# Four one-bank PSUM tiles in place of two two-bank tiles for the products of a kernel's second network, with a new instruction order

## The chip, the cores and the metric

The kernel runs on one core of a Trainium2 chip. The metric is the device time in microseconds (us) of one execution, and the time of a kernel is the median over its runs. The engines are TensorE (PE: matmuls; PEld is its weight load), VectorE (DVE), ScalarE (ACT), GpSimd (POOL) and SyncE (SP, which issues every DMA here). Matmuls write PSUM, a memory of eight banks; one bank holds 128 x 512 fp32. DVE and ACT read PSUM; POOL works on SBUF only.

## What is computed

Windowed attention feeds a first gated network, and that a second one; only the second is changed.

```python
# x: 1536 tokens x 512, from the first network
h = x @ w_in                       # 512 -> 2048
relu6 = np.clip(h + 3.0, 0.0, 6.0)
g = h * relu6 / 6.0
return (g @ w_out).astype(np.float32)   # 2048 -> 512
```

## The kernel before

Every matmul is done in two-part fp32: an operand is split into a high part and a remainder (`split`, lines 286 to 325: ACT or DVE copies the high part, POOL or DVE subtracts), and three matmuls of 128 x 512 give one product. The tokens are three chunks of 512. The second network goes in four rounds of four f-tiles (128 of the 2048 hidden columns each). In a round, chunks 0 and 1 go two f-tiles at a time through a fast scheme with seven products in place of eight (`strassen`): a product is six matmuls into one PSUM bank (`product`, line 806), and DVE at once adds the bank to a sum in SBUF (`plus`, line 889; the first is a copy, lines 894 and 895). Chunk 2 goes plainly (`single2`, line 937): two products of twelve matmuls into the two halves of one tile. So there are 56 products of six and 16 of twelve, 72 in all, and four banks for them. `act2` is the gate: ACT `Relu` into `t` (line 818), DVE `min` and multiply (819), ACT copy to the high part of `g` (821), POOL or DVE the remainder (825). For chunk 2 it takes both halves, 128 x 1024, in one instruction each. `second2` (line 848) multiplies `g` by the output weights into the banks `y0` to `y3`, three matmuls a time, and DVE adds those to `part` (863). `convert` and `weights2` (lines 305 to 313, 790) turn float64 weights, loaded by DMA, into fp32 and form differences of them.

In the first network `first_product` (line 637) and `second_product` (654) do the same jobs, with another gate (lines 701 to 745); `evac` (672) and 679 pass its result on. Attention is in lines 349 to 603.

The four product banks are two tiles, `hb0` and `hb1`, each of two banks (`pair_of`). The framework that places semaphores knows tiles: an instruction that writes or reads a tile is kept in order with the accesses to it that were recorded ahead of it. The planner inside the kernel (`Plan`) keeps its books by single banks, `("h", 0)` to `("h", 3)`; it decides nothing about semaphores.

The order is a table: `ORDER` lists all operations in the order in which they are given out, each engine runs its own in that order, and `PICK` says for an operation that can run on several engines which one does it.

Of the kernel before, what the change touches and what calls it, by code (L numbers as in the profile page):

```python
# [22 lines left out]
P = 128  # L23
# [6 lines left out]
N = 512  # L30
# [33 lines left out]
    "#P%-'##M$$$X#Q$#%.&3%3&1&W%5&,#R#Y#S%4#L%0%/%6%8&*%1'K%X'I%7%;%9%R&V&+%<%:%Y&2%=&'&-&>#.'J&4&.*X'L&5"
    "&/&?'M#T$%&@&D'D'N'$&A&(&I(,&X'%&E';+.&F#/&G&B)8&H*Y':+$&J&K#U*Z')&L&C&M&N+%+2&6&P&O&Q'*+/+#&R'<+&'."
    "+3+<+0&Z&S'++1'/+4+'&T+((-',+5'&+)'0+=(/(.'1+*'2+J)#+6''+@'-'((H++'5+A+>'3+7'6+?+,'=+B(M+8+-,$+C'V(N"
    "(%+K'>'A'O+D+9(O'B+N(I+E(J+L,#+F'4+M+O+Z+:'?'7+G,(+;+Q'@+Y(P+P'8+X+H'9'W+R,2(&+I(',5'C+S'X'E(Y(Q'Y(K"
    "'Z(L,4):'G,%)9,D(#,&'F,3),+T(T(R($)',F)-+U).(:,G(Z,',6(((U'P,+)(()))(S'R(0'Q+V'S(V(1+W,7(2)/,),E(W,:"
    ",W(X(;1L(*,V,*)0(<)$)*,;)+(='T,H(>'U,,)%(?)&)>(@(3,<)1,8)3)2,Y)4)C,X,-)5,.,I(+,L,Z)?)D,9)E(A)6,/(4)7"
    ",J)@,M,=,K);,N-#,>(6)A-4,0)Q,?)O-&,1)=(5)<,O)B)F-'-1-51M,@-3)G-0,A,P)H-(-$-8-2(7,B)J(D-F)I,C)Z,Q-%(8"  # L70
    ',R-)-9-E(9)U)K-D*#,S*$-B-:(B)L-*(C-+-X,T*.-,1Z-G*%)P-6,U1S---J(E)M-T-H-Y-C1O(F-I*/-K-U1N)N.$-W(G-L-.'
    ")R-7-M-/2).%.6-;*0)T-N*&-<)V)S*9)W)X2%)Y-V.&*)-=.0**-O.:*'-P./*(2,.1.7->*4*+1T-Q..*:*,*5-?.H-R1P-Z-@"
    ".;.2*-.#.3-A.4*1.I*6*;.5.8.<.L.E*<-S*2.'.G.9.(.F*=.M.=.W*7.)2#.Z.>*3*G*8.N.?.*.X/&.@.D/#.A*@*L.Y.+.V"
# [125 lines left out]
def tile_kernel(ctx, tc, qT, kT, kw, vw, vt, w1, w2, av, bv, masks, ident, blk, out):  # L199
# [22 lines left out]
    sp = [ExitStack() for _ in range(2)]  # L222
# [536 lines left out]
    def bank_at(n):  # L759
        return pair_of(n // 2)[:, n % 2, :]  # L760
# [50 lines left out]
    def act2(src, reads, in_psum, two, g, gk):  # L811

        n = t_used[0] % 4
        t_used[0] += 1 + two
        a, v = n // 2, (slice(0, 2) if two else n % 2)
        t = t2[a][:, v]
        tk = [("t", a, w) for w in ((0, 1) if two else (n % 2,))]
# [3 lines left out]
        add(ACT, 0.96 if two else 0.53, lambda: nc.scalar.activation(g[:, 0], t, AF.Copy), tk, gk)  # L821
        for w in range(1 + two):
            def rest(eng, w=w):
                ts, gs = (t[:, w], g[:, :, w]) if two else (t, g)
                eng.tensor_tensor(out=gs[:, 1], in0=ts, in1=gs[:, 0], op=ALU.subtract)  # L825

            add(POOL, 1.26, lambda f=rest: f(nc.gpsimd), tk[w:w + 1], gk[w:w + 1], port=True,
                more=[(DVE, 0.61, lambda f=rest: f(nc.vector), True)])
# [40 lines left out]
    def strassen(r, m):  # L869
# [241 lines left out]
```

## Time and profile before

| | us |
|---|---|
| median of 3 runs (lowest, highest) | 600.57 (599.98, 600.9) |
| the profiled execution: its own time | 601.33 |
| its span, first to last instruction | 599.5 |
| PE busy in the span | 584.6 (98%) |
| DVE busy | 496.5 (83%) |
| ACT busy, POOL busy | 352.2, 288.5 |

Busy time of PE is that of matmuls, which overlap, so what counts is the pace from one start to the next. The profiled execution took 0.76 us more than the median.

### The profile page before, as it was taken

The page shows a single profiled execution, that of the slowest core. Times are in us where ns is not written, and L with a number is a line of the kernel's source. Part 1 is how long each engine was busy: PE and PEld are TensorE (multiplying, and loading weights), DVE is VectorE, ACT ScalarE, POOL GpSimd, SP SyncE. Part 2 cuts the span into 40 slices and gives each one's busy share as a digit, 9 for nine tenths or more (in the row PEclk, how much of TensorE's full clock was granted, in tenths as well). Part 3 has the DMA queues.
Part 4 walks back from the last instruction along what each step waited for, and adds up shares of the span by engine and source line. Part 5 has one row for each costly group of instructions (what it writes and reads, how often), then busy time and mean ns, then how long its engine had stood idle before and what let it go on. Part 6 is the DMA issues. An engine that isn't in the chain of part 4 may idle for free.

```text
span 599.5 us, 9595 instructions
## 1 busy us (share of the span) xinstructions
PE 584.6 (98%) x3613; PEld 466.1 (78%) x3613; DVE 496.5 (83%) x874; ACT 352.2 (59%) x637; POOL 288.5 (48%) x269
## 2 busy tenths in 40 slices
PE   8999999999999999999999999999899999999997
PEld 4477888888888888888888778787678888778886
DVE  5999999989999999978999889747797868568653
ACT  3999989999677777846665454324640433233410
POOL 2688655462554535465666645242523066254400
PEclk9999999999999999999999999999899999999999
DMA  8967631501331313100001300320412024002005
GB/s 314 361 238 240 229 113 68 172 1 34 107 105 36 106 36 134 43 2 0 35 1 37 112 29 28 112 71 1 140 35 106 1 72 140 1 1 71 0 2 210
DMA packets 17982, 53.10 MB, mean 89 GB/s; under 512 B 2272, under 2 KB 2784, under 8 KB 17936
## 3 DMA queue, kind: packets, MB, share of 16 engines
q1 hardware_dynamic: 17936, 52.49, 25.3%
q8 instruction: 28, 0.46, 0.3%
q14 instruction: 18, 0.15, 0.1%
HBM read 48.55 MB, written 3.15 MB: 86 GB/s over the span
## 4 chain that ended last, share of the span: by engine, by line
PE 82%; DVE 8%; POOL 4%; issue 2%; ACT 2%; DMA 1%; SPq 0%; DVEq 0%; POOLq 0%; ACTq 0%
PE y L654 22%; PE y L848 15%; PE hb L637 15%; PE hb L806 11%; PE hs L637 8%; PE hb L937 6%; PE hs L574 2%; PE hs L507 2%; PE hs L591 2%; DVE q L889 1%; DMA mask_sb<-in_masks 1%; POOL g L825 1%; DVE raw L313 1%; POOL wt L325 1%; DVE t L819 1%
## 5 line engine op out<-in xcount | busy, mean ns | idle before, releaser
L654 PE MATMUL y<-g,wt 128*128 128x512 f32 x576 | 138.9, 392 | 0.0
L654 PEld LDWEIGHTS y<-g,wt 128*128 128x128 f32 x576 | 107.0, 188 | 22.2 <-POOL g L745 0.3
L848 PE MATMUL y<-wt,g 128*128 128x512 f32 x480 | 118.0, 391 | 0.3 <-DVE wt L325 0.2
L848 PEld LDWEIGHTS y<-wt,g 128*128 128x128 f32 x480 | 90.4, 189 | 20.0 <-DVE wt L325 0.5
L637 PE MATMUL hb<-xx,wt 128*128 128x512 f32 x384 | 89.6, 389 | 0.0
L325 POOL TENSOR_TENSOR wt<-raw,wt 128x512 fp32r<-128x512 f32 x38 | 53.3, 1407 | 63.9 <-ACT wt L286 47.2
L637 PEld LDWEIGHTS hb<-xx,wt 128*128 128x128 f32 x384 | 72.0, 188 | 15.3 <-DVE t L737 0.3
L286 ACT ACTIVATE wt<-raw 128x512 fp32r<-128x512 f32 x55 | 36.4, 670 | 40.9 <-DVE raw L313 16.0
L305 POOL TENSOR_SCALAR raw<-raw 128x512 f32<-128x512 f32 x50 | 38.2, 774 | 44.6 <-DMA raw<-in_w 44.3
L309 ACT ACTIVATE raw<-raw 128x512 f32<-128x512 f32 x62 | 40.3, 668 | 30.4 <-POOL raw L305 29.7
L825 POOL TENSOR_TENSOR g<-t,g 128x512 fp32r<-128x512 f32 x21 | 29.5, 1411 | 53.3 <-ACT g L821 50.8
L821 ACT ACTIVATE g<-t 128x512 fp32r<-128x512 f32 (+1 forms) x32 | 23.2, 735 | 47.3 <-PE y L848 33.8
L313 DVE SCALAR_TENSOR_TENSOR raw<-raw 128x512 int32<-128x512 int32 x62 | 47.2, 765 | 3.2 <-ACT raw L309 2.7
L717 POOL TENSOR_TENSOR q<-q,u 128x512 f32<-128x512 f32 x28 | 38.6, 1392 | 23.2 <-ACT u L707 12.6
L806 PE MATMUL hb<-wt,wt 128*128 128x512 f32 x192 | 48.6, 393 | 0.9 <-DVE q L889 0.8
L637 PE MATMUL hs<-xx,wt 128*128 128x512 f32 x192 | 48.0, 398 | 0.0
L937 PE MATMUL hb<-xx,wt 128*128 128x512 f32 x192 | 46.5, 394 | 0.7 <-DVE q L889 0.5
L745 POOL TENSOR_TENSOR g<-t,g 128x512 fp32r<-128x512 f32 x22 | 31.7, 1445 | 26.5 <-ACT g L739 22.5
L937 PEld LDWEIGHTS hb<-xx,wt 128*128 128x128 f32 x192 | 36.4, 191 | 9.3 <-DVE q L889 1.2
L806 PEld LDWEIGHTS hb<-wt,wt 128*128 128x128 f32 x192 | 35.6, 188 | 10.2 <-issue 0.9
L806 PE MATMUL hb<-xx,wt 128*128 128x512 f32 x144 | 37.7, 398 | 5.2 <-DVE q L889 3.1
L863 DVE SCALAR_TENSOR_TENSOR part<-y,part 128x512 f32<-128x512 f32 x36 | 24.2, 685 | 22.4 <-PE y L848 22.4
(174 smaller groups left out, 1100.2 us busy)
## 6 DMA issues: line engine op xcount, KB each, us to landing
raw<-in_w SPq DMA_DIRECT2D x62, 512.0 KB, 4.3
vv<-in_vw SPq DMA_DIRECT2D x6, 512.0 KB, 7.3
out<-part SPq DMA_DIRECT2D x12, 256.0 KB, 2.9
k<-in_kT SPq DMA_DIRECT2D x4, 384.0 KB, 4.3
q<-in_qT SPq DMA_DIRECT2D x6, 256.0 KB, 7.8
e<-in_kT SPq DMA_DIRECT2D x4, 384.0 KB, 6.6
raw<-in_vt SPq DMA_DIRECT2D x3, 512.0 KB, 6.8
e<-in_vw SPq DMA_DIRECT2D x3, 512.0 KB
```

The costliest lines, as they stand in the source:

```text
L286: nc.scalar.activation(out_, in_, AF.Copy)
L305: eng.tensor_scalar(out=hif, in0=hif, scalar1=CAP, scalar2=-CAP, op0=ALU.min, op1=ALU.max)
L309: add(ACT, 0.58, lambda: nc.scalar.activation(hif, hif, AF.Prelu, scale=REBIAS, alpha=2.0 ** 32), [kr], [(kr, 1)])
L313: add(DVE, 0.61, lambda: nc.vector.scalar_tensor_tensor(out=lo, in0=hi, scalar=3, in1=lo, op0=ALU.logical_shift_left, op1=ALU.bitwise_or), ...
L325: eng.tensor_tensor(out=to()[:, 1], in0=src, in1=to()[:, 0], op=ALU.subtract)
L637: mm(ps, lt, rt, start=(k == 0), stop=(k == 11))
L654: mm(y, lt, rt, start=(i == 0 and j == 0), stop=(i == HALF - 1 and j == 2))
L717: eng.tensor_tensor(out=q2[a][:, w], in0=q2[a][:, w], in1=u2[:, w], op=ALU.mult)
L806: mm(bank_at(bank_), left(lp, kk), right(rp, kk), start=(j == 0), stop=(j == 5))
L825: eng.tensor_tensor(out=gs[:, 1], in0=ts, in1=gs[:, 0], op=ALU.subtract)
L848: mm(yb[d], lt, rt, start=(j == 0 and e == 0), stop=(j == QUART - 1 and e == 2))
L937: mm(pair_of(a)[:, u, :], w_at(n)[:, lp, kk * P:(kk + 1) * P], x_of(2)[:, rp, kk, :], start=(j == 0), stop=(j == 11))
```

## The change

The banks become four tiles `hc0` to `hc3` of one bank each, made where the second network first touches a pair, after the pair tile is closed. Chunk 2's gate is done for each f-tile by itself. `PICK` and `ORDER` are replaced whole; a line of each stands for them.

```diff
 PICK = (
-    '0001230000110000000010000000000011111011001100000100010011000000000000000001001000101001100000000000'
+    '0000230000000000001100111010000000011100001100000000000001000000110000000101110000001010000000000010'
...
 ORDER = (
-    "###)#4#(#;#$#6#2#0#8#%%>#9%Z#5#&#:#7%E#'#3#<#1#?#V$&%?#W#@$(%@$'$.&#%A#*$7%B$)$/&%$0%F$9#=%L%G$H$*$1"
+    "###(#4#)#;#$#2#6#0#8#%%>#9#:#5#&%E#3#<#'#7#W#1%Z#V$&%?#?#B$(%@$7$'$.%A%F$8#=$)#@$9#A%L%H$Y%G$*$/%B$0"
...
@@ pair_of
-            hq = ctx.enter_context(tc.tile_pool(name=f"hq{a}", bufs=1, space=PSUM, reuse_waits="tile", side=SIDES[a]))
+            hq = hs2[a].enter_context(tc.tile_pool(name=f"hq{a}", bufs=1, space=PSUM, reuse_waits="tile", side=SIDES[a]))
...
     def bank_at(n):
-        return pair_of(n // 2)[:, n % 2, :]
+
+        def make():
+            hs2[n // 2].close()
+            hr = ctx.enter_context(tc.tile_pool(name=f"hr{n // 2}", bufs=1, space=PSUM, reuse_waits="tile", side=SIDES[n // 2]))
+            return [hr.tile([P, N], F32, name=f"hc{2 * (n // 2) + u}") for u in range(2)]
+
+        return keep(("hc", n // 2), make)[n % 2]
...
-    def act2(src, reads, in_psum, two, g, gk):
+    def act2(src, reads, in_psum, g, gk):
...
-        add(ACT, 1.02 if two else 0.55, lambda: nc.scalar.activation(t, src(), AF.Relu, bias=lnb[:, 2:3]), [*reads, "lnb"], tk)
-        add(DVE, 1.14 if two else 0.61, lambda: nc.vector.scalar_tensor_tensor(
+        add(ACT, 0.5 if in_psum else 0.62, lambda: nc.scalar.activation(t, src(), AF.Relu, bias=lnb[:, 2:3]), [*reads, "lnb"], tk)
+        add(DVE, 0.61, lambda: nc.vector.scalar_tensor_tensor(
...
-                        mm(pair_of(a)[:, u, :], w_at(n)[:, lp, kk * P:(kk + 1) * P], x_of(2)[:, rp, kk, :],
+                        mm(bank_at(2 * a + u), w_at(n)[:, lp, kk * P:(kk + 1) * P], x_of(2)[:, rp, kk, :],
...
-        act2(lambda: pair_of(a), [("h", 2 * a), ("h", 2 * a + 1)], True, 1, g2[b], [("g", b, u) for u in range(2)])
         for u in range(2):
-            second2(r, 2, 2 * m + u, (g2[b][:, :, u, :], [("g", b, u)]))
+            place_ = g_place()
+            act2(lambda u=u: bank_at(2 * a + u), [("h", 2 * a + u)], True, *place_)
+            second2(r, 2, 2 * m + u, place_)
```

In the changed kernel lines 806, 848, 889 and 937 are 812, 850, 891 and 939; lines 818, 819, 821 and 825 are 822, 823, 825 and 828; 790 is 796.

**First place, PE in the first round of the second network.** `wt1`, `wt2`, `wt6` and `wt7` hold sums of activations, `wt0` and `wt5` differences of weights, `xx0` to `xx2` the three chunks. Before, from the product with `wt1`:

```order
L806 MATMUL hb0_2020<-wt1_471,wt0_360 128x512 x6
L806 MATMUL hb0_2020<-xx1_117,wt0_360 128x512 x6
L806 MATMUL hb0_2020<-xx0_115,wt3_463 128x512 x6
L806 MATMUL hb1_1964<-wt2_600,wt9_2000 128x512 x6
L806 MATMUL hb1_1964<-wt7_1238,wt5_1075 128x512 x6
L806 MATMUL hb0_2020<-wt1_471,wt5_1075 128x512 x6
L848 MATMUL y0_81<-wt8_1958,g1_80 128x512 x3
L806 MATMUL hb1_1964<-xx0_115,wt3_463 128x512 x6
```

The first three go to halves 1, 0 and 1 of `hb0`. Now, at the same products:

```order
L812 MATMUL hc0_3208<-xx1_117,wt0_361 128x512 x6
L654 MATMUL y2_83<-g0_79,wt5_1061 128x512 x3
L654 MATMUL y3_84<-g0_79,wt5_1061 128x512 x3
L654 MATMUL y0_81<-g0_79,wt5_1061 128x512 x3
L654 MATMUL y1_82<-g0_79,wt5_1061 128x512 x3
L812 MATMUL hc3_3160<-wt2_411,wt9_1990 128x512 x6
L812 MATMUL hc1_3209<-xx0_115,wt3_463 128x512 x6
```

Each bank has a name of its own, and twelve matmuls of the first network have moved in between.

**The same place on DVE.** Before, the additions that read those products:

```order
L325 TENSOR_TENSOR wt5_1075<-raw1_71,wt5_1075 128x512
L889 TENSOR_TENSOR q1_77<-hb0_2020,q0_76 128x512
L889 TENSOR_TENSOR q1_77<-hb1_1964,q1_77 128x512
L672 SCALAR_TENSOR_TENSOR part12_118<-y1_82,part12_118 128x512
L889 TENSOR_TENSOR q0_76<-hb1_1964,q0_76 128x512
L889 TENSOR_TENSOR q1_77<-hb0_2020,q1_77 128x512
```

The second row reads the product with `wt1` (half 1 of `hb0`), the last the product with `xx1` (half 0). Now:

```order
L891 TENSOR_TENSOR q0_76<-hc3_3160,q0_76 128x512
L891 TENSOR_TENSOR q1_77<-hc1_3209,q0_76 128x512
L891 TENSOR_TENSOR q0_76<-hc0_3208,q0_76 128x512
L325 TENSOR_TENSOR wt2_411<-part0_116,wt2_411 128x512
```

The additions stand together, and none shares a tile with a later product.

**Second place, PE and DVE where chunk 2 has its first turn.** PE before, from the last products of the Strassen pair:

```order
L806 MATMUL hb1_1964<-xx1_117,wt5_1075 128x512 x6
L848 MATMUL y1_82<-wt9_2000,g1_80 128x512 x3
L937 MATMUL hb0_2020<-xx2_119,wt8_1958 128x512 x12
L937 MATMUL hb0_2020<-xx2_119,wt9_2000 128x512 x12
L937 MATMUL hb1_1964<-xx2_119,wt4_663 128x512 x12
```

PE now:

```order
L939 MATMUL hc0_3208<-xx2_119,wt8_1956 128x512 x12
L939 MATMUL hc1_3209<-xx2_119,wt9_1990 128x512 x12
L812 MATMUL hc2_3159<-wt2_411,wt4_667 128x512 x6
L850 MATMUL y3_84<-wt9_1990,g1_80 128x512 x3
L812 MATMUL hc3_3160<-xx1_117,wt5_1061 128x512 x6
L939 MATMUL hc2_3159<-xx2_119,wt3_463 128x512 x12
```

Two Strassen products now stand between those of chunk 2, and `hc2` is written again nine matmuls after its last product. DVE now, from the read that frees `hc1` to the one that frees `hc2`:

```order
L891 TENSOR_TENSOR q0_76<-hc1_3209,q0_76 128x512
L828 TENSOR_TENSOR xx1_117<-t0_74,xx1_117 128x512
L311 TENSOR_SCALAR raw3_73<-raw3_73 128x512
L823 SCALAR_TENSOR_TENSOR t0_74<-t0_74,q0_76 128x512
L313 SCALAR_TENSOR_TENSOR raw2_72<-raw2_72 128x512
L325 TENSOR_TENSOR wt8_1956<-raw1_71,wt8_1956 128x512
L796 TENSOR_TENSOR raw1_71<-raw2_72,raw1_71 128x256
L325 TENSOR_TENSOR wt9_1990<-raw2_72,wt9_1990 128x512
L891 TENSOR_TENSOR u_78<-hc2_3159,u_78 128x512
```

Seven instructions of other jobs stand between the two reads.

## Rows read from the trace of the kernel before

**Rows 1.** Page, part 1: busy us (share of the span) x instructions.
```profile
PE 584.6 (98%) x3613; PEld 466.1 (78%) x3613; DVE 496.5 (83%) x874; ACT 352.2 (59%) x637; POOL 288.5 (48%) x269
```

**Rows 2.** Busy time by stretch: first network, its end, second network.
```profile
core 0: us, PE busy (x) PEld busy (x) DVE busy (x) ACT busy (x) POOL busy (x), PEclk, DMA share, GB/s
60.00:310.00 250.00, 250.00 (x1598) 205.15 (x1597) 234.29 (x388) 192.97 (x332) 134.71 (x118) 1.00 0.22 73
310.00:340.00 30.00, 30.00 (x134) 24.86 (x133) 26.89 (x35) 18.18 (x25) 18.98 (x15) 1.00 0.07 20
340.00:582.00 242.00, 234.98 (x1012) 189.42 (x1011) 177.47 (x256) 92.38 (x140) 95.82 (x85) 0.99 0.17 57
```

**Rows 3.** Timeline of PE: start us, us, matmuls; in brackets idle before, releaser.
```profile
309.30 12.40 PE L654 MATMUL y<-g,wt 128*128 128x512 f32 x54
321.54 1.52 PE L806 MATMUL hb<-xx,wt 128*128 128x512 f32 x6
...
339.22 1.52 PE L806 MATMUL hb<-xx,wt 128*128 128x512 f32 x6
341.53 1.67 PE L806 MATMUL hb<-xx,wt 128*128 128x512 f32 x6 [0.78 <-DVE q L889]
343.54 4.50 PE L806 MATMUL hb<-wt,wt 128*128 128x512 f32 x18 [0.34 <-DVE q L889]
...
349.76 1.65 PE L806 MATMUL hb<-xx,wt 128*128 128x512 f32 x6 [1.04 <-DVE u L889]
```

**Rows 4.** Timeline of DVE, the same place.
```profile
340.78 1.42 DVE L889 TENSOR_TENSOR q<-hb,q 128x512 f32<-128x512 f32 x2 [2.21 <-PE hb L806]
```

**Rows 5.** Waits of PE from 300 us on: us in total, times, longest us.
```profile
PE hb L806 <- DVE q L889: 3.9, 5, 2.1
PE hb L806 <- DVE u L889: 2.0, 2, 1.0
...
PE y L848 <- DVE wt L325: 0.2, 1, 0.2
```

**Rows 6.** Busy time by stretch, columns as in rows 2.
```profile
426.00:429.00 3.00, 3.00 (x10) 2.33 (x9) 1.90 (x4) 1.53 (x3) 1.15 (x2) 0.61 0.44 157
429.00:432.00 3.00, 3.00 (x12) 2.38 (x12) 3.00 (x6) 2.96 (x5) 1.18 (x1) 0.82 0.12 44
```

**Rows 7.** Groups by form: count | busy us, mean ns of one | idle before, its releasers.
```profile
L313 DVE SCALAR_TENSOR_TENSOR raw<-raw 128x512 int32<-128x512 int32 x62 | 47.2, 765 | 3.2 <-ACT raw L309 2.7
L311 DVE TENSOR_SCALAR raw<-raw 128x512 int32<-128x512 int32 x62 | 36.9, 604 | 1.8 <-DMA raw<-in_w 1.7
L325 DVE TENSOR_TENSOR wt<-raw,wt 128x512 fp32r<-128x512 f32 x40 | 33.0, 827 | 5.1 <-ACT wt L286 4.6
L889 DVE TENSOR_TENSOR q<-hb,q 128x512 f32<-128x512 f32 x35 | 23.8, 684 | 19.3 <-PE hb L806 13.9 <-PE hb L937 3.5 <-ACT u L894 1.8
L819 DVE SCALAR_TENSOR_TENSOR t<-t,q 128x512 f32<-128x512 f32 x22 | 19.8, 905 | 0.5 <-ACT t L818 0.4
L825 DVE TENSOR_TENSOR g<-t,g 128x512 fp32r<-128x512 f32 x19 | 14.9, 792 | 0.5 <-ACT g L821 0.4
L790 DVE TENSOR_TENSOR raw<-raw,raw 128x256 f32<-128x256 f32 x10 | 5.8, 581 | 6.5 <-POOL raw L790 4.2 <-POOL wt L325 2.3
L819 DVE SCALAR_TENSOR_TENSOR t<-t,hb 128x1024 f32<-128x1024 f32 x8 | 9.7, 1216 | 4.9 <-ACT t L818 4.9
L818 ACT ACTIVATE t<-hb,lnb 128x1024 f32<-128x1024 f32 x8 | 9.0, 1119 | 9.2 <-DVE g L825 6.3 <-PE hb L937 2.0 <-POOL g L825 0.9
L821 ACT ACTIVATE g<-t 128x1024 fp32r<-128x1024 f32 x8 | 8.5, 1059 | 27.5 <-PE y L848 27.5
L821 ACT ACTIVATE g<-t 128x512 fp32r<-128x512 f32 x24 | 14.8, 627 | 19.8 <-DVE t L819 13.5 <-PE y L848 6.3
```

**Rows 8.** Waits of PE over the whole span, columns as in rows 5.
```profile
PE y L507 <- DVE stat L552: 1.8, 1, 1.8
PE hs L349 <- DVE z L347: 1.2, 1, 1.2
```

More of the change, by code (lines that the diff above doesn't have):

```diff
@@ L64 @@
[L64 to L73, printed above, removed]
@@ new lines @@
+    "+<&S+3(-+''/(/+1(.&T#U+('B+4'&'++=+)'0+5',+*'-+J+@'1''+6'2'((H++'5+A+>'3+7'6+?+,'=+B(M(I+-,$+C'V'>+8"
+    "'D+K(%+D+9'O'4+E+L'7+F+N+M(N+:+X+O'8(O,#+G(J+Q+;+Y'W,%'A+R+Z(P'Y,&'?'X,4'@'9'C+H(&,5(Z'Z,('P)#,2+I('"
+    ")8'E(#(K+P(L(Q,3'G($'Q,E'F),(T(:,G(():(0(R(U+S,D(S'R,F)'+T(V'S+U(1,6()+V)()-,'(*).+W))(W'T(;)*)/,),X"
+    "(2,:(X,Y(<(=)0)$,+,*)+(>'U,H)%,,)&,7(+(3)>,;,-,8(A)1)3(?,V)2)4(@,L,W,<)C)5)?,.,/,Z,9)6,I)@)D(6)E,0)7"
+    ",J,=,M,K)A,>);,N)F,?,1,O-4)<)Q-#)O-&,@1Z)B)G)9)=(B-',P-1,A(C-2-(-5-$)J-8)P(D-3(4-%1L-0(5,Q)H,B-F-9)I"
@@ new lines @@
+    ',C)K-:-),R)Z(E(7-B-*,S)L-J-+-E,T*#-,-G-C,U)M(8-X-K)U-6)N--*$*%-7-D(9-Y)R.$)V-L)W1S-H-..%1M-;-U)X1O-I'
+    "(F)S-W-<-T2%1N(G)T.6-M*&)Y2)-=*.-N*0-/*9-V->-O*'.1-?*(*).7-P...:-Q.0***:.&*/*;*4./-Z1P*+.8.;-R.H.#*<"
+    ".<-@*,-A.'*-*5.22*1V*1.31T.(.4*6.L.Z*=*21U*3*G-S.).I*@*7.F/#.**8.5.X.+/&.E.9*L/'.D.M*>.J.W2#.=.V.K.>"
+    '*H*M.N.G.,*?*A.Y*I.?2$/4*N.O.@.-.P.A*O.Q*B/5.R/$.S/3*E.B/%/(*F/1*C*J2&/8/2/6.T/F/9*K*P*D.C/)2,/*/7*S'
+    "/0/+*T.U2+*Q/C1W*R/G/E/,/;*U/-/J/H/D/</I*V/W1Q*W/V1X/:1R/B/./K/X/M/=2I2'///N2-/>2./Y/L/O/?/P/@/U0&/Q"
@@ new lines @@
+    "0#2(0*052L2W0'/R0+0(0,/S0%060)2J/A0-2/0./T2X3&2K0/0$1Y0G0900080C2P/Z2Y010D0:070H020F0=0<0I0E0;030>0?"
+    "2Z0J0R3)2M0K3#2N0L0@0S2O3$040A3'0M3%0U1$0N0T3X1(1%0X3J0Y0O1)1&143(1*3Y2Q0Q1'132R0B1+0P4#0V1,3*0Z1=1-"
+    "0W1A1#1>1.153K181?161/1<1:1B10193Z1@11203L1C121D3M2S171E4$222T211F2U4%3+1G3,1H1;2:4&4'263N2>3-2V4U1I"
+    '3O1J1K2;2?3.3P2=2<4G2@253Q3;293?4X3/3<232A3>3@242B273A4V323=302C284H3B332D31374(4I342E4W353C4Y364J4.'
+    '2F4K3D382G4L393E4M4)414/3F2H:<4*3G3R4+3S3T5+4Z4,484-5#3H5$4<:R42493I5,3U3:4:4=3V4;4>43553W465945564N'
@@ new lines @@
+    "5.4?5:40584@475;5/5%504A5754534B:=5<445&4O5-4C5=514Q524D:U5>5D4F5?:S4E:T5@5E4P5'5A4R:?5B5(6%5N5R5O4S"
+    "5S6&:>4T5P5C:C5T5H:@6?5I5)5L5Q5*6;5G5U6@5F6<:Y5J5V:V5M6=5W5K6*6>6A6'6.:Z:D6B6)5X6(6C6,5Y;#6-6+655Z6J"
+    '6D6#686$6/6E606K616F627+6T6G6U6H7,6I696V6X6W6Y6O75;$6M:F79766Z6Q6L787:7#7.72777;7$6S707%7<6N6R637&7='
+    "6P747'667-:E647(716:7D7)7>7*7?7E:A7@:B:G8%:J:H7N:I7O7R:K8&:L;%:M7S7Q7T7/8767737P:N7I7A:O7F7U;(7G7C7B"
+    "7K7V7J887H8;7W7M8:7L8<8(898=8)8,;)7X8>8'8*7Y8?8-8+;+7Z818G8/828$8@838A8F8#8B:$:*9'8P:+:0:,8T8Q8U9(;*"
@@ L105 @@
+    "E=E(GYELF=EMG=EGF?E<F8EFE,G;G>FUE6G<E7GEEOF9GVGFF:E>G?GIH%FXEHE?EIF@GCG@EQGDGXH#ESFAGNH$EPFYG'H'I,FZ"
+    'G#GZGGH,H-EUH(G$H&G%H*GJETGKGPGHH.GLGTH/ENGOG(I-G*G)H)G&H0H+G+H4H?G,H8GSI.H9I>H5ERH1H2GMH3GQG-H>GRHB'
+    'H:H=H6H;HHI6HCH<H7H@HNHDHRI/I?I7HJHLIHHOIIHAHSHFI8HPI@I9I0HWIAI1HMHVI#HZHQI(HUHYHTI&HXI*IBI3ICI$IJI;'
+    "IKI%I4I+HII2HKI5I)HGI<I'HEI:IEI=IFINIMITIDIRIUILISIGIPIOIQIVIW"
 )
@@ L221, in tile_kernel @@
     yb = [pp.tile([P, N], F32, name=f"y{i}") for i in range(4)]
-    sp = [ExitStack() for _ in range(2)]
+    sp, hs2 = [[ExitStack() for _ in range(2)] for _ in range(2)]
     hp = [sp[i].enter_context(tc.tile_pool(name=f"hp{i}", bufs=1, space=PSUM, side=SIDES[i])) for i in range(2)]
@@ L809, in product, with rest @@
         add(PE, 1.362, go, reads, [("h", bank_)], fresh=(("h", bank_),))
-    def act2(src, reads, in_psum, two, g, gk):
+    def act2(src, reads, in_psum, g, gk):
         n = t_used[0] % 4
[L814 to L817, printed above, removed]
-        add(ACT, 1.02 if two else 0.55, lambda: nc.scalar.activation(t, src(), AF.Relu, bias=lnb[:, 2:3]), [*reads, "lnb"], tk)
-        add(DVE, 1.14 if two else 0.61, lambda: nc.vector.scalar_tensor_tensor(
-            out=t, in0=t, scalar=6.0, in1=src(), op0=ALU.min, op1=ALU.mult), reads, tk, port=not in_psum)
[L821 to L828, printed above, removed]
+        t_used[0] += 1
+        t, tk = t2[n // 2][:, n % 2], [("t", n // 2, n % 2)]
+        add(ACT, 0.5 if in_psum else 0.62, lambda: nc.scalar.activation(t, src(), AF.Relu, bias=lnb[:, 2:3]), [*reads, "lnb"], tk)
+        add(DVE, 0.61, lambda: nc.vector.scalar_tensor_tensor(
+            out=t, in0=t, scalar=6.0, in1=src(), op0=ALU.min, op1=ALU.mult), reads, tk, port=not in_psum)
+        add(ACT, 0.53, lambda: nc.scalar.activation(g[:, 0], t, AF.Copy), tk, gk)
+        def rest(eng):
+            eng.tensor_tensor(out=g[:, 1], in0=t, in1=g[:, 0], op=ALU.subtract)
+        add(POOL, 1.26, lambda: rest(nc.gpsimd), tk, gk, port=True, more=[(DVE, 0.61, lambda: rest(nc.vector), True)])
     def temp_place():
@@ L909, in strassen @@
         first = [g_place() for _ in range(2)]
-        act2(lambda: c11, k11, False, 0, *first[0])
-        act2(lambda: c12, k12, False, 0, *first[1])
+        act2(lambda: c11, k11, False, *first[0])
+        act2(lambda: c12, k12, False, *first[1])
         if m == 0:
@@ L914, in strassen @@
             for e in range(2):
-                act2((lambda: c21, lambda: c22)[e], (k21, k22)[e], False, 0, *second[e])
+                act2((lambda: c21, lambda: c22)[e], (k21, k22)[e], False, *second[e])
             for e in range(2):
@@ L920, in strassen @@
             for e in range(2):
-                act2((lambda: c21, lambda: c22)[e], (k21, k22)[e], False, 0, *second[e])
+                act2((lambda: c21, lambda: c22)[e], (k21, k22)[e], False, *second[e])
             for e in range(2):
@@ L1027, in tile_kernel, with bank_now @@
     second_network()
+    def bank_now(kind, n):
+        if kind == "y":
+            return yb[n]
+        return bank_at(n) if ("hc", n // 2) in made else pair_of(n // 2)[:, n % 2, :] if ("hb", n // 2) in made else hs[n]
     with tc.manual_schedule():
@@ L1038, in tile_kernel @@
                 for _ in range(times):
-                    mm(yb[n] if kind == "y" else bank_at(n) if ("hb", n // 2) in made else hs[n], z[:, :P], z, start=True, stop=True)
+                    mm(bank_now(kind, n), z[:, :P], z, start=True, stop=True)
             plan.ops[i][2]()
```

66 lines of the change are left out of this document (25 added, 41 removed).

## The prediction

> **What bounds the kernel now.** The page's first part says that PE is busy 98% of the span, the next engine, DVE, 83% [rows 1]. Such a busy share hides drawn-out matmuls, so I read pace instead. On the timeline of PE, 54 matmuls take from 309.30 to 321.54 us, 12.24 us or 0.2267 us each [rows 3]; that is the pace at which PE runs when nothing holds it. Then the stretches: from 60 to 310 us PE has no idle time at all, and from 310 to 340 none either [rows 2]. In the second network, 340 to 582 us, 1012 matmuls took 242.0 us; at pace they need 1012 x 0.2267 = 229.4 us [rows 2, 3]. So **12.6 us are lost there**, more than the 7.0 us by which PE's busy time falls short of the stretch.
>
> The waits of PE say on what: 3.9 and 2.0 us in seven waits of a product (L806) for a DVE addition (L889), and 0.2 us for a weight [rows 5]. They understate the loss. The block at 339.22 has six matmuls and should hand over at 340.58; the next starts at 341.53, which is 0.95 us late, with 0.78 named. That one needs 1.36 us and has 2.01 until the next, 0.65 late with 0.34 named [rows 3]. And after the longest wait, 2.1 us, the granted clock was 0.61 and 0.82, so part of those 6 us ran at the lower of the two levels, 1.2 GHz; 22 matmuls took 6.0 us instead of 5.0, another 1.0 us [rows 6].
>
> Why is the addition late? Take the first wait, with the order of before at the first place. The product with `wt1` goes to one half of `hb0` and ends when the block with `xx1` begins, at 339.22. DVE then stands idle, 2.21 us in all, and starts the addition that reads it only at 340.78, which is when the matmuls with `xx1`, into the *other* half, have ended (339.22 + 1.52 = 340.74) [rows 3, 4]. PE's next product starts when this addition is over. So both sides wait for the neighbour's bank: the tile has two banks and one history. The group of additions has the same reading in sum: 19.3 us of DVE idle time ahead of them, 13.9 and 3.5 of it put down to products [rows 7]; much of this is plain waiting for work, so it prices nothing. Read from the built program, 21 of the 72 products wait for a read of the other half of their tile, and 20 reads wait for a later product into the other half. In the changed one none does.
>
> **The change part by part.**
>
> *Four tiles.* This takes away the wait for the neighbour. At most it returns 12.6 us. What stays is a bank's own handover: DVE reads it in 0.684 us [rows 7], with 0.04 us to start (340.74 to 340.78 above), so some 0.8 us or 3.5 matmuls when DVE is free at once. Counted in the new order, no bank that an addition has to free is written again sooner than 6 matmuls (1.36 us) after its last product, and 5 of those 60 rewrites come within 12 (2.7 us); before, 4 did. PE is safe there if DVE is on time, and DVE runs in order. The second place is such a case. From the end of the read that frees `hc1` DVE has L828, L311, L823, L313, L325, L796, L325 and the addition to do: 0.79 + 0.60 + 0.91 + 0.77 + 0.83 + 0.58 + 0.83 + 0.68 = 5.99 us at the means of the same operations [rows 7]. PE, from its start on `hc1` to its next product into `hc2`, has 12 + 6 + 3 + 6 = 27 matmuls, 6.12 us. The two meet within 0.13 us, so one instruction that is late by half its length makes PE wait. I let each of the five tight rewrites cost one foreign instruction's lateness of 0.55 us (an estimate: the lightest two in that list are 0.58 and 0.60), 2.7 us in all. From below the bound is nothing; from above it is the whole 12.6 us, 0.175 us on each of 72 products.
>
> *Chunk 2's gate by single f-tiles.* Eight pairs of instructions become sixteen on each engine. DVE: 16 x 0.684 (the nearest read of one bank) less 9.7 is +1.2 us. ACT's copy: 16 x 0.627 less 8.5 is +1.5 us. ACT's `Relu` on one bank has no row; it lies between half the wide one, 0.56, and the wide one, 1.12 us, and the copy's narrow form costs 0.59 of its wide one, so I take 0.66 us, +1.6 us (bounds 0 and +8.9) [rows 7]. The cover is slack: ACT works 92.4 of 242.0 us here and DVE 177.5 [rows 2]; in a stretch of 232 us they would be at 41% and 77%. Charged: nothing; if DVE had no slack, 1.2 us. In return the first half's gate can begin after its own product, 12 matmuls or 2.7 us earlier, and frees its bank by itself.
>
> *Order and picks.* PE has the same matmuls in both programs, product by product, and as many that only fill (25). By count DVE gives six of the multiplications of line 717 to POOL in the first network and takes seven clamps of line 305 from it; PE had no idle time there, so nothing is to be won. In the attention part the planner issues scores and loads in another sequence. PE's waits there are 1.8 and 1.2 us [rows 8]: the first could go or double, the second waits for the first memset and stays. I take 0, bounds -1.8 and +1.8. The end has the same shape: one output bank after another, an addition, a store.
>
> **Sum.** 12.6 - 2.7 = 9.9 us less: 601.33 - 9.9 = 591.4 us for an execution like the profiled one, which stood 0.76 us above the median of the runs shown. So 590.7 us.
>
> **The rivals.**
>
> *A, the handover is late more often.* The additions wait on ACT and POOL as well as on PE, and without the forced pauses DVE has less time to catch up. For it: the spare 0.13 us above, and DVE at 90% just ahead, 26.9 of 30 us [rows 2]. Against it: over 242 us DVE has a quarter free. If half the loss stays, 6.3 us, the time is 601.33 - 6.3 - 0.76 = 594.3; the case reaches from 593.5 to 599.4.
>
> *B, nothing changes.* The products took turns on four banks before as well, and if DVE's own lateness were the cause, tiles would not matter: 600.6 us. The Trainium skill (Perfetto Trace Analysis, section "Matmuls") says that independent groups should rotate through different PSUM banks so that the evacuation of one overlaps the next group's matmuls; by that rule alone this kernel was already right. The trace disagrees: DVE was idle, not late, ahead of the addition at 340.78 [rows 4].
>
> *C, slower.* Place: the first network, where DVE works 234.3 of 250 us, 94% [rows 2]. The new table arranges its gates anew; if they come late, PE, which lost nothing there, loses. It decides from 9.9 us on, 0.2 us on each of the 48 f-tile steps. If DVE came to idle as much again as its 15.7 us, all on PE's path, the time would be 590.7 + 15.7 = 606.4 us. For it only the small reserve; against it, that DVE's load there gets lighter on balance of the counts above.
>
> *D, more than forecast.* No rewrite late and 1.8 us won at the start: 601.33 - 12.6 - 1.8 - 0.76 = 586.2; the case is everything below 588.
>
> **How the numbers follow.** Forecast (588 to 593.5) 0.62, A 0.20, D 0.07, B 0.04, C 0.07. From 587 to 597 lie the forecast's own range, some 0.14 of A and 0.04 of D, together 0.8; the range takes in the bound of no late rewrite (588.0) and of half the loss with 1.8 us lost at the start (596.1). A measurement of this kernel can tell about 0.2%, 1.2 us, from no change: faster 0.62 + 0.20 + 0.07 = 0.89, same 0.04, slower 0.07.
>
> **What would show it.** Right: in the second network about 2.7 us above 0.2267 us a matmul; no long wait of a product on an addition, and DVE starting an addition when its own product ends; no dip of the granted clock there; ACT's narrow `Relu` near 0.66 us and neither ACT nor DVE nearer to full; the first network still without idle time on PE. Wrong: products still waiting, now with DVE busy ahead of the addition (A); the same waits with DVE idle (B); PE idle between 60 and 310 us (C).

## The result and the profile after

The changed kernel takes 589.87 us (median of 4 runs, 588.89 to 591.61) beside 600.28 us for the kernel before (4 runs, 599.48 to 600.9) on the same chip: a ratio of 0.983, 95% interval 0.9802 to 0.9859. The profiled execution took 589.21 us, with a span of 587.4 us; before it was 601.33 and 599.5.

The page's first part after the change, which answers to [rows 1]:

```profile
PE 578.6 (98%) x3608; PEld 466.6 (79%) x3613; DVE 494.4 (84%) x887; ACT 348.5 (59%) x648; POOL 294.7 (50%) x272
```

PE's share is 98% both times, so it tells nothing of the gain. The stretches do; columns as in [rows 2], the last one cut where the program now ends:

```profile
60.00:310.00 250.00, 249.91 (x1605) 204.83 (x1595) 231.63 (x375) 190.81 (x331) 154.46 (x133) 1.00 0.22 73
310.00:340.00 30.00, 30.00 (x134) 24.70 (x133) 29.59 (x40) 16.22 (x22) 17.97 (x16) 1.00 0.08 24
340.00:572.00 232.00, 232.00 (x1025) 192.12 (x1024) 176.29 (x282) 93.34 (x156) 82.53 (x70) 1.00 0.17 59
```

In the second network PE has no idle time and the clock is at its full level: 1025 matmuls in 232.0 us, which is the pace (1025 x 0.2267 = 232.4). The first network is as tight as before. Of the waits of PE over the whole span only some at the start are left, the two largest of them here. None is on a product bank; before there were eight, the seven of [rows 5] and one of a product of chunk 2 (L937, 0.5 us):

```profile
PE hs L1045 <- issue: 1.4, 4, 0.9
PE hs L349 <- DVE z L347: 1.2, 1, 1.2
```

PE's timeline, with the first product, the second place and the last output block (the brackets that [rows 3] had are gone):

```profile
322.46 1.55 PE L812 MATMUL hc<-xx,wt 128*128 128x512 f32 x6
...
353.13 5.60 PE L939 MATMUL hc<-xx,wt 128*128 128x512 f32 x24
358.57 1.52 PE L812 MATMUL hc<-wt,wt 128*128 128x512 f32 x6
359.93 0.84 PE L850 MATMUL y<-wt,g 128*128 128x512 f32 x3
360.61 1.52 PE L812 MATMUL hc<-xx,wt 128*128 128x512 f32 x6
361.97 2.88 PE L939 MATMUL hc<-xx,wt 128*128 128x512 f32 x12
...
570.05 13.76 PE L850 MATMUL y<-wt,g 128*128 128x512 f32 x60
```

Two rows of this view give a measure that is the same for every kernel below: the time from the first product of the second network to the start of the last output block. Here it is 570.05 - 322.46 = 247.59 us. Between them lie 1092 matmuls in the new order (1089 in the old, whose last block has 63); at 0.22667 us each [rows 3] they need 247.52 us, so 0.1 us is lost. Before, from 321.54 [rows 3] to 581.47 us, it was 259.93, of which 13.1 lost. That is 13.0 us won; the first product begins 0.92 us later; 12.1 us is the difference of the spans.

The groups by form that answer to [rows 7]:

```profile
L891 DVE TENSOR_TENSOR q<-hc,q 128x512 f32<-128x512 f32 x35 | 23.5, 683 | 7.9 <-PE hc L812 7.6
L823 DVE SCALAR_TENSOR_TENSOR t<-t,hc 128x512 f32<-128x512 f32 x16 | 10.7, 681 | 4.7 <-ACT t L822 4.7
L822 ACT ACTIVATE t<-hc,lnb 128x512 f32<-128x512 f32 x16 | 10.7, 678 | 9.2 <-PE hc L939 5.8 <-DVE g L828 1.9 <-POOL g L828 1.4
L825 ACT ACTIVATE g<-t 128x512 fp32r<-128x512 f32 x40 | 25.0, 628 | 49.4 <-PE y L850 43.4 <-DVE t L823 3.1 <-DVE u L891 2.9
```

The additions of this form take what they took, but DVE's idle time ahead of them is 7.9 us instead of 19.3, and none of it is for a product of chunk 2 any more. The narrow `Relu` takes 0.678 us.

### The profile page after: what moved, and what is told of

The parts are those of the page before. It is cut to its first block, busy times and chain, and to the rows that moved or that the text cites. A ratio compares the mean times of both kernels' runs of the same rounds, so it can differ in the third digit from the quotient of the medians.

```text
span 587.4 us, 9645 instructions
## 1 busy us (share of the span) xinstructions
PE 578.6 (98%) x3608; PEld 466.6 (79%) x3613; DVE 494.4 (84%) x887; ACT 348.5 (59%) x648; POOL 294.7 (50%) x272
## 4 chain that ended last, share of the span: by engine, by line
PE 94%; DMA 2%; DVE 1%; SPq 1%; issue 1%; POOL 0%; ACT 0%; DVEq 0%
PE y L654 23%; PE y L850 22%; PE hb L637 15%; PE hc L812 13%; PE hs L637 8%; PE hc L939 7%; PE hs L591 2%; PE hs L507 2%; PE hs L574 1%; DMA mask_sb<-in_masks 1%; DMA k<-in_blk 1%; SPq L280 1%; DVE s L520 0%; POOL s L549 0%; PE hs L434 0%
## 5 line engine op out<-in xcount | busy, mean ns | idle before, releaser
L637 PE MATMUL hb<-xx,wt 128*128 128x512 f32 x384 | 89.5, 389 | 0.0
L325 POOL TENSOR_TENSOR wt<-raw,wt 128x512 fp32r<-128x512 f32 x44 | 62.4, 1425 | 51.0 <-DVE wt L322 30.4
L637 PEld LDWEIGHTS hb<-xx,wt 128*128 128x128 f32 x384 | 72.1, 188 | 15.0
L717 POOL TENSOR_TENSOR q<-q,u 128x512 f32<-128x512 f32 x34 | 46.2, 1368 | 23.8 <-ACT u L707 14.4
L825 ACT ACTIVATE g<-t 128x512 fp32r<-128x512 f32 x40 | 25.0, 628 | 49.4 <-PE y L850 43.4
L812 PE MATMUL hc<-wt,wt 128*128 128x512 f32 x192 | 47.4, 389 | 0.0
L939 PE MATMUL hc<-xx,wt 128*128 128x512 f32 x192 | 45.6, 389 | 0.0
L939 PEld LDWEIGHTS hc<-xx,wt 128*128 128x128 f32 x192 | 36.0, 188 | 7.5
L812 PEld LDWEIGHTS hc<-wt,wt 128*128 128x128 f32 x192 | 36.0, 188 | 7.5
L637 PEld LDWEIGHTS hs<-xx,wt 128*128 128x128 f32 x192 | 35.1, 188 | 7.7 <-issue 0.2
```

What stands on the lines that cost most here:

```text
L325: eng.tensor_tensor(out=to()[:, 1], in0=src, in1=to()[:, 0], op=ALU.subtract)
L637: mm(ps, lt, rt, start=(k == 0), stop=(k == 11))
L717: eng.tensor_tensor(out=q2[a][:, w], in0=q2[a][:, w], in1=u2[:, w], op=ALU.mult)
L812: mm(bank_at(bank_), left(lp, kk), right(rp, kk), start=(j == 0), stop=(j == 5))
L939: mm(bank_at(2 * a + u), w_at(n)[:, lp, kk * P:(kk + 1) * P], x_of(2)[:, rp, kk, :], start=(j == 0), stop=(j == 11))
```

## The experiments

**Theory 1**: two banks in one tile are kept in order with each other, and this is the loss. **Theory 2**: the new order and picks make the gain, and the tiles alone do nothing. **Theory 3** (rival A): the handover of a bank is late anyway, so little is to be had. Each run stands beside the kernel before on its own chip.

### Tiles and order, crossed

`e1_pair_new_order` keeps the new order, the new picks and the split gate, but the four banks are halves of two tiles again:

```diff
...
 def bank_at(n):
-    def make():
-        ...
-    return keep(("hc", n // 2), make)[n % 2]
+    return pair_of(n // 2)[:, n % 2, :]
```

> The changed kernel with one thing undone: the four product banks are halves of two tiles again; the new order, the new picks and the gate by single f-tiles stay. If the shared tile is the cause, the loss comes back, 12 us or so, since the new order was laid out for separate banks too: 598 to 605 us, with products waiting for DVE additions, DVE idle ahead of them, and some 10 us or more lost in the second network. If the new order and picks are the cause, it stays at about 590 us. If the single gate is, the same.

`e2_four_old_order` has the four tiles and the split gate, with the table of before; the two halves of each gate stand one behind the other where the wide one stood:

```diff
 PICK = (
-    '0000230000000000001100111010000000011100001100000000000001000000110000000101110000001010000000000010'
+    '0001230000110000000010000000000011111011001100000100010011000000000000000001001000101001100000000000'
...
```

> The old order and the old picks with the four tiles; each wide operation of the gate stands as its two halves, one behind the other, in the old place. If the shared tile is the cause, most of the loss is gone here as well: 588 to 593 us, and PE keeps its pace in the second network. If the new order is the cause, about 600 us. The start is the old one, so PE's first large matmul begins at about 39.6 us.

`e3_pair_old_order` has both edits, so that of the change only the split gate is left.

> The old order, the old picks and the two shared tiles, with the gate by single f-tiles alone. If the shared tile is the cause: about as before, 598 to 603 us, since the narrow gate's extra 1 to 3 us on DVE and ACT are covered and its halves still share a tile. If the narrow gate itself gives the gain, 590 to 595 us.

The stretch is that from the first product to the last output block, read from PE's timeline; lost is what it has above its matmuls at pace.

| kernel | tiles | order | stretch, us | lost, us | median, us | ratio to before |
|---|---|---|---|---|---|---|
| before | two | old | 259.93 | 13.1 | | |
| e3 | two | old | 260.38 | 13.5 | 601.04 | 0.9992 (0.9981 to 1.0003) |
| e1 | two | new | 260.05 | 12.5 | 602.65 | 1.0022 (1.0006 to 1.0038) |
| e2 | four | old | 247.70 | 0.9 | 590.54 | 0.9814 (0.9795 to 0.9834) |
| changed | four | new | 247.59 | 0.1 | 589.87 | 0.983 (0.9802 to 0.9859) |

With the same tiles, the order changes the stretch by 0.5 us at most; from two tiles to four, 12 to 13 us go in either order. Theory 2 falls: the new order on shared tiles is 0.2% slower than the kernel before, the old order on four tiles has the whole gain. In e1 the waits of PE from 300 us on are as follows (L933 is `single2`, L885 the additions, L890 and L891 the copy that a sum begins with, on ACT and on DVE, L817 the gate's `min` and multiply):

```profile
PE hb L933 <- DVE q L885: 2.5, 3, 1.4
PE hb L806 <- DVE t L817: 2.0, 2, 1.6
PE hb L806 <- DVE q L885: 1.0, 2, 0.5
PE hb L806 <- ACT q L890: 0.8, 1, 0.8
PE hb L806 <- DVE u L891: 0.6, 1, 0.6
```

These are nine waits with 6.9 us named, at other places than in [rows 5], for 12.5 us lost. The other side of it is the waits of DVE from 320 to 590 us:

```profile
DVE q L885 <- PE hb L806: 9.8, 8, 3.0
...
DVE q L885 <- PE hb L933: 5.1, 2, 3.8
```

DVE waits 14.9 us for products, and PE waits for DVE's reads: that both wait for each other is what one history for two banks does. DVE's idle time by itself shows nothing. In the changed kernel the first of these rows is 8.1 us and in e2 it is 12.5, and in neither is a wait of PE for an addition named from 300 us on; the row of e2:

```profile
DVE q L891 <- PE hc L812: 12.5, 8, 5.4
```

### One pair shared, one apart

`e4_one_pair` shares a tile between banks 2 and 3 only:

```diff
...
 def bank_at(n):
+    if n // 2 == 1:
+        return pair_of(1)[:, n % 2, :]
...
```

> The changed kernel with banks 2 and 3 as halves of one tile and banks 0 and 1 separate. If the loss belongs to the shared tile, a part near half of what the two pairs cost: 593 to 599 us, and every long wait of a product is on the tile that is shared. If what counts is something else that the shared tiles bring about, such as a load on DVE, the waits fall on the separate banks as well.

It took 597.77 us, a ratio of 0.9937 (0.9922 to 0.9952). The stretch is 254.94 us (323.44 to 578.38), of which 7.4 are lost: six tenths of the 12.5 of e1, where half the sharing by itself would give half. The expectation that every long wait is on the shared tile failed, since the longest wait of PE is on a bank that stands apart:

```profile
PE hc L814 <- DVE t L825: 1.6, 1, 1.6
PE hb L941 <- DVE q L893: 0.8, 1, 0.8
```

The timelines of DVE and, below, of PE say why:

```profile
366.30 0.69 DVE L893 TENSOR_TENSOR q<-hb,q 128x512 f32<-128x512 f32 x1 [3.75 <-PE hb L941]
...
371.17 0.69 DVE L825 SCALAR_TENSOR_TENSOR t<-t,hc 128x512 f32<-128x512 f32 x1 [0.36 <-ACT t L824]
```

```profile
361.88 1.66 PE L814 MATMUL hb<-xx,wt 128*128 128x512 f32 x6
363.38 2.88 PE L941 MATMUL hb<-xx,wt 128*128 128x512 f32 x12
...
371.91 1.45 PE L814 MATMUL hc<-xx,wt 128*128 128x512 f32 x5 [1.57 <-DVE t L825]
```

DVE stood idle for 3.75 us, from 362.55 us on, ahead of an addition. The last Strassen product ahead of it (361.88) had handed over at 363.38; the rest of the wait was for the twelve matmuls of chunk 2 into the other half of the shared tile, which the addition doesn't read. What was behind it in DVE's queue came late, and with it the gate's read of `hc`, a bank with a tile of its own; PE then waited for that. So the sharing is paid at separate banks too, by way of the queue.

### How much the handover can bear

Theory 3 asks how near the additions are to being late. Stores of zeros to a tile that holds zeros are put on DVE ahead of each of the 56 additions:

```diff
 def plus(to, bank_, other, reads, writes):
...
+    def go():
+        for _ in range(1):          # 2 in e10, 3 in e6
+            nc.vector.memset(z, 0.0)
+        nc.vector.tensor_tensor(out=to, in0=bank_at(bank_), in1=other, op=ALU.add)
...
```

The banks that a copy or a gate frees are delayed only by way of DVE's queue.

> The changed kernel with one needless DVE instruction (a memset of 128x256 words, some 0.27 us) in front of each of the 56 additions that free a product bank, 15 us of DVE work in all. If the handover of the banks is as tight as the prediction counted (0.13 us to spare at the second place, five such rewrites), PE now waits at these and at some more: 2 us or more above the changed kernel, 592 to 596 us. If DVE has slack and PE is ahead of its need nearly everywhere, less than 1 us: 589.5 to 591 us.

> The same with three such instructions in front of each addition, 45 us of DVE work in the second network, which would fill DVE to some 95% there. Tight handover: 0.8 us late at each of 56 additions, PE waits at most rewrites that come within 18 matmuls (10 of them) and wherever DVE falls behind: 10 us or more above the changed kernel, 600 us and up. Slack: some 3 to 8 us, 593 to 598 us, since DVE's queue now runs late as a whole but the banks' reserve of up to several us takes most of it.

They gave 593.31 us (ratio 0.988, 0.9843 to 0.9917) and 623.98 us (1.0378, 1.0348 to 1.0408), both in the ranges expected of a tight handover; where the time went was not what was expected, as shown below. The profiled execution of e5 had lost 2.1 us ahead of the first store already, so the changed kernel was run again beside one store and two:

> The changed kernel itself, run beside the next two on one chip, since its four runs (588.9 to 591.6 us) spread as wide as the effect of one inserted instruction. Theory (four tiles leave PE unhindered in the second network): from the first product of the second network to the start of the last output block, which the first profile put at 322.46 and 570.05 us, again 247.6 us within 0.5; what differs between runs lies ahead of the first product, in the attention part. Rival (the second network itself varies by run): the same stretch differs by 1 us or more while the start agrees.

> One store to a constant ahead of each of the 56 additions, as before. Its first profile was 4.4 us above the changed kernel's, but 2.1 us of this lay ahead of the first inserted instruction. Theory (handover with about a quarter microsecond to spare at a few places): 2 to 3 us more than the changed kernel run beside it, all after the first product, in one or two waits. Rival (each addition's lateness counts): 56 x 0.27 = 15 us more. Rival (no effect, the first run only started late): within 1 us of the changed kernel.

> Two stores ahead of each addition, 0.5 us on each. One cost some 2 us in the second network, three cost 33. Theory (slack at single places is used up one after the other, DVE still has some 20% free over the whole stretch): between 5 and 15 us above the changed kernel, with waits of products on additions at several places. Rival (a threshold: DVE falls behind for good once its queue is near full): 20 us or more, waits everywhere, granted clock below 1 in places. Rival (slack is large): under 4 us.

What a store adds is read from the timeline of DVE. With one (e9), a store and its addition repeat every 0.82 us, where two additions in a row stand 0.60 apart in the changed kernel:

```profile
352.50 0.27 DVE L893 MEMSET z<- 128x256 uint32 x1
352.70 0.62 DVE L894 TENSOR_TENSOR q<-hc,u 128x512 f32<-128x512 f32 x1
353.32 0.27 DVE L893 MEMSET z<- 128x256 uint32 x1
```

That is 0.22 us, less than the 0.27 of its row. With two the repeat is 1.21 us (354.92 to 356.13 in e10) and with three 1.60 us (362.65 to 364.25 in e6): 0.61 and 1.00 us more for each addition. The second store adds more than the first because it begins 0.39 us after it, while an addition begins 0.20 us after a store; that the stores wait for each other because they write one tile was not tested. The sums over 56 additions in the table are estimates from these repeats.

| stores | added to each addition, x 56 | stretch, us | paid in it | median, us | ratio to before |
|---|---|---|---|---|---|
| none (e8) | 0 | 247.60 | 0 | 590.12 | 0.9809 (0.9796 to 0.9823) |
| one (e9; e5) | 0.22, 12.3 | 249.94; 249.90 | 2.3 | 593.72; 593.31 | 0.9884 (0.9865 to 0.9903); 0.988 |
| two (e10) | 0.61, 34 | 261.52 | 13.9 | 607.1 | 1.0087 (1.0068 to 1.0106) |
| three (e6) | 1.00, 56 | 281.08 | 33.5 | 623.98 | 1.0378 (1.0348 to 1.0408) |

Of what is added, 19, 41 and 60% is paid: of the first 12.3 us four fifths are hidden, of the last 22 almost 90% is not. With one store there is one named wait in the second network, the same in e5 and e9, and it is not on a bank (e9):

```profile
PE y L850 <- POOL g L828: 1.2, 1, 1.2
```

The stores and additions push back the sums from PSUM behind them (L672), those the work of ACT, that the copy to the high part of `g`, that POOL's remainder, and PE waits for `g`. POOL's timeline in e9 has that last link; ACT's copy ahead of it began at 349.75 us, in the changed kernel at 347.04, with the first product only 1.2 us earlier:

```profile
350.45 1.77 POOL L828 TENSOR_TENSOR g<-t,g 128x512 fp32r<-128x512 f32 x1 [1.31 <-ACT g L825]
```

The stores themselves are the smaller part of this lateness. When that work reaches L672 it is 0.7 us late (342.02 us against 340.17, less the 1.2). Then an L325 on DVE takes 1.72 us where it took 0.80, and POOL's remainder above takes 1.77 where it took 1.30; e9 first, then the changed kernel:

```profile
342.61 1.72 DVE L325 TENSOR_TENSOR wt<-raw,wt 128x512 fp32r<-128x512 f32 x1
```

```profile
340.77 0.80 DVE L325 TENSOR_TENSOR wt<-raw,wt 128x512 fp32r<-128x512 f32 x1
```

Beside this L325 POOL does another remainder. In the changed kernel POOL began second, at 341.08 us, and took 1.66 us; in e9 it began first, at 342.49, and took 1.29. The rows suggest that the one that comes second is drawn out; no run tests it.

The banks are late too with one store, by less than the views name as a wait. At the second place the 24 matmuls into `hc0` and `hc1` take 5.77 us to the next start, where they took 5.44 in the changed kernel. The twelve into `hc0` are over at 358.54 us (355.82 + 12 x 0.22667), and the read that frees `hc1` ends at 358.68 (PE in e9, then DVE):

```profile
355.82 5.94 PE L943 MATMUL hc<-xx,wt 128*128 128x512 f32 x24
361.59 1.52 PE L812 MATMUL hc<-wt,wt 128*128 128x512 f32 x6
```

```profile
358.06 0.62 DVE L894 TENSOR_TENSOR q<-hc,q 128x512 f32<-128x512 f32 x1
```

In the changed kernel this read ends at 355.57 us, and PE's matmuls into `hc1` begin at 355.85. So 0.28 us are to spare there.

With two stores the banks are what PE waits for most, at this same handover first of all; the longest group of waits of PE in e10 from 300 us on, and the wait at that place in its timeline:

```profile
PE hc L943 <- DVE q L894: 4.8, 3, 2.6
```

```profile
362.61 3.02 PE L943 MATMUL hc<-xx,wt 128*128 128x512 f32 x12 [2.57 <-DVE q L894]
```

So the mechanism of theory 3 is there, and the changed kernel stays just below it: 0.28 us at one handover, which a single store on each addition uses up, since their lateness adds up in DVE's queue. The expected 5 to 15 us for two stores hold for the stretch (13.9) and not for the medians, which stand 17.0 us apart; the profiled execution of e10, 604.54 us, is the fastest of its six.

### The old front with the new rest

`e7_old_start_new_rest` takes the first 1000 operations, with their picks, in the order of before, and the rest as in the changed kernel:

```diff
 ORDER = (
-    "###(#4#)#;#$#2#6#0#8#%%>#9#:#5#&%E#3#<#'#7#W#1%Z#V$&%?#?#B$(%@$7$'$.%A%F$8#=$)#@$9#A%L%H$Y%G$*$/%B$0"
+    "###)#4#(#;#$#6#2#0#8#%%>#9%Z#5#&#:#7%E#'#3#<#1#?#V$&%?#W#@$(%@$'$.&#%A#*$7%B$)$/&%$0%F$9#=%L%G$H$*$1"
...
```

> The changed kernel whose first 1000 operations (attention and the first part of the first network) stand in the old order and with the old picks; the rest is the new order. If the new start costs the 0.8 us that the traces show between the two (the same matmuls before the second network end that much later), it gives this back: 588.5 to 590 us, a difference that the runs can hardly tell. If the start is no matter, as the changed kernel.

It took 588.57 us (5 runs, 588.34 to 589.53), a ratio of 0.9797 (0.9771 to 0.9824). The first product begins at 321.69 us and the stretch is 247.58 us, so it has the front of the one and the second network of the other. Its span, 586.6 us, is the shortest here; by the ratios it can't be told from the changed kernel (0.983, 0.9802 to 0.9859, and in e8 0.9809, 0.9796 to 0.9823).

## Why the prediction was right, step by step

**What bounds the kernel, and the cause: right.** The loss was in the second network, and it came from two banks with one history: in e1 the loss is there with all else changed, in e2 it is gone with the order unchanged. The 12.6 us counted from 340 us on are 13.1 from the first product on. The stretch at the lower clock is gone as well. It had cost more than the 1.0 us worked out from [rows 6], whose two windows count matmuls that reach over their edges: from 425.61 to 432.12 us 21 matmuls took 6.51 us, at pace 4.76. The sum doesn't change by this, since it counts the loss as a whole.

**What stays, 2.7 us: mis-sized; it is 0.1 us** (0.9 in the old order, e2). The step was "I let each of the five tight rewrites cost one foreign instruction's lateness of 0.55 us", and behind it stood the second place with 5.99 us of DVE work against 6.12 us of PE. PE's part was exact (355.85 us, the middle of the 24 matmuls, to 361.97). DVE's part in the changed kernel's timeline:

```profile
354.89 0.68 DVE L891 TENSOR_TENSOR q<-hc,q 128x512 f32<-128x512 f32 x1
355.49 0.72 DVE L828 TENSOR_TENSOR xx<-t,xx 128x512 fp32r<-128x512 f32 x1
356.14 0.42 DVE L311 TENSOR_SCALAR raw<-raw 128x512 int32<-128x512 int32 x1
356.47 0.68 DVE L823 SCALAR_TENSOR_TENSOR t<-t,q 128x512 f32<-128x512 f32 x1
357.07 0.68 DVE L313 SCALAR_TENSOR_TENSOR raw<-raw 128x512 int32<-128x512 int32 x1
357.68 0.68 DVE L325 TENSOR_TENSOR wt<-raw,wt 128x512 fp32r<-128x512 f32 x1
358.39 0.43 DVE L796 TENSOR_TENSOR raw<-raw,raw 128x256 f32<-128x256 f32 x1
359.46 0.69 DVE L325 TENSOR_TENSOR wt<-raw,wt 128x512 fp32r<-128x512 f32 x1 [0.64 <-ACT wt L286]
360.13 0.69 DVE L891 TENSOR_TENSOR u<-hc,u 128x512 f32<-128x512 f32 x1
```

From 355.57 to 360.82 it is 5.25 us with 0.64 of idle time, so 4.6 of work, and `hc2` is free 1.15 us early instead of 0.13; 0.28 of this is that the read ahead of it ended before PE began on `hc1`, which the prediction had taken to fall together. The handover of `hc1` is the nearer one, as the stores showed, and the prediction didn't look at it. Two things were read wrongly in [rows 7]: the rows are 1.0 us shorter in sum than the means, and they overlap by 0.4. The means are pulled up by a few long instructions: in the second network of before, where one line is asked for by itself, the view gives least, median and most, and the median of L311 is 0.42 us, not 0.60, that of L819 0.69, not 0.91:

```profile
L311 DVE TENSOR_SCALAR raw<-raw x26: 413/423/1532, 347.2 to 552.2; 128x512 int32<-128x512 int32 x26
L819 DVE SCALAR_TENSOR_TENSOR t<-t,q x21: 673/686/1800, 348.0 to 573.3; 128x512 f32<-128x512 f32 x21
```

And rows overlap: an instruction of 0.68 us is followed by the next after 0.60, so a sum of rows counts some 0.08 us twice where one follows at once. The Trainium skill (Perfetto Trace Analysis, section "DVE / Act Engine Instruction (TENSOR_ADD, Activation, etc)") says that the end of a row is the acknowledgement of the last write, and that the next instruction may begin to fetch when the one before has finished executing; this trace agrees, with the 0.08 us.

**The split gate, nothing: right.** The narrow `Relu` took 0.678 us (taken: 0.66), the copy 0.628, the `min` 0.681. DVE is at 176.3 of 232.0 us, 76%, and ACT at 40% (77 and 41 were worked out). e3, which has this edit alone, differs from before by less than a run can tell.

**Order and picks, 0 with bounds of 1.8 either way: right for the first pair of profiles, and made of two parts.** The second network loses 0.8 us less in the new order (0.1 against 0.9). The front is later: the first product begins at 321.49 to 322.00 us in the four profiled executions with the old front (before, e2, e3, e7) and at 322.33 to 324.57 us in the eight with the new one; the means are 321.68 and 323.48. So the upper bound, 1.8 us, is what the front costs on average, though in the first pair of profiles it was 0.92; only there do the two parts come to nothing. Part of it lies in the first network: in e1, e5 and e10 PE waits there for gates, 1.1 to 1.2 us in two waits, which none of the four with the old front has. The five others with the new front wait for no gate there and begin at 323.07 us on average, 1.4 us later than with the old front. Their PE is busy 249.88 us or more of the 250 from 60 to 310 us, so this part lies ahead of that, where attention runs; it was not followed further. The waits come and go between executions with the same front. For these bounds the prediction took two waits from [rows 8]; there are five ahead of the second network, 4.2 us in all.

**The rivals.** A: there is no such wait in the changed kernel; the stores show that one handover is 0.28 us from it. B is refuted by e1 against the changed kernel: the banks take turns alike in both, and the stretches are 12.5 us apart. The Trainium skill (Perfetto Trace Analysis, section "Matmuls") says that independent groups should rotate through different PSUM banks; here that was worth something only when the rotation was by tiles, which is what the semaphores know. C: the first network has PE at 249.91 of 250 us and DVE at 231.6, less than before; the gates that come late in e1, e5 and e10 are its mechanism, at 1.1 to 1.2 us. D comes near with the front where it was: by sum 601.33 - 13.0 - 0.76 = 587.6, but the kernel that has this front, e7, measured 588.57, just above D's 588.

**The sum.** 9.9 us were forecast and 12.1 came: 13.1 of loss instead of 12.6, less 0.1 instead of 2.7, less 0.9 at the front instead of 0. This is between the profiled executions; between the medians of the result it is 10.4, since the profiled one stood 1.05 us above the median before and 0.66 below it after. That the forecast median of 590.7 is within 0.8 us of the measured 589.87 is in part luck: the 2.6 us charged too much for the rewrites were partly made up by a front that was charged at nothing and by this spread.

## What to carry to other kernels

Where two banks that are filled and read in turn lie in one tile, look for both engines waiting for each other: a matmul that waits for a read of the half it doesn't write, and the reader idle until a product that it doesn't read has ended. An idle reader alone is no sign. Give each bank that is handed over by itself a tile of its own before touching the order. To know whether a handover is near its limit, take starts from the timeline and medians, not means of groups, and put a store of known price in front of it: the share that does not come through is hidden by slack. Then look where the rest is paid, since it can be at another engine than the one that was delayed.

## What was not expected of the hardware

The granted clock doesn't follow the length of a wait alone. At the second place PE waited 2.57 us in e10 and 2.52 us in e6, before the same product; in the windows behind, the clock was 1.00 in e10 (first row) and 0.50, 1.2 GHz, the lower of the two levels, in e6 (second row). In e6 PE had waited 2.00 us some 10 us earlier as well, and the clock behind that was 0.62 (355 to 358 us); in e10 that earlier wait was 1.32 us, with 1.00 behind it. What decides was not tested.

```profile
364.00:367.00 3.00, 3.00 (x15) 2.48 (x14) 2.37 (x5) 0.66 (x1) 0.00 (x0) 1.00 0.00 0
```

```profile
366.00:369.00 3.00, 3.00 (x7) 2.39 (x8) 2.96 (x6) 1.25 (x2) 0.00 (x0) 0.50 0.02 5
```

And a wait costs a little more than its length: the block of six behind it takes 1.50 us to the next start instead of 1.36 (355.13 - 353.63 in e10), 0.14 us. It is the same in [rows 3], where the two blocks of six that waited have rows of 1.67 and 1.65 us and the others 1.52.
